# Batch 0's output product as seven half-size products, another order of its units, two later loads, and scores over 128 rows

## The chip, the cores and the metric

The kernel runs on one core of a Trainium2 chip. The metric is the device time of one execution in microseconds (us). TensorE (PE) multiplies matrices, VectorE (DVE), ScalarE (ACT) and GpSimd (POOL) work elementwise, and SyncE (SP) issues most of the DMAs. Each of them works through its own instructions in the order of the program.

## What is computed

```python
mask = q_bucket[:, :, :, None] == k_bucket[:, :, None, :]   # 6 sign bits of q @ proj, of k @ proj
scores = np.where(mask, scale * q @ k.T, -1e9)
attn = softmax(scores) @ v                  # 4 batches, 8 heads, 768 x 64
x = attn.transpose(0, 2, 1, 3).reshape(3072, 512)
h = x @ w_in                                # 512 x 2048
out = (h * sigmoid(h)) @ w_out              # 2048 x 512
```

Everything is float32 at the edges; the kernel multiplies in float16.

## The kernel before

**Attention in slots.** Two heads make a pair, two pairs a quad (`Q`), four pairs a batch. Each head is cut into `NU = 9` score blocks, so the main loop (line 735) has 288 slots `w`, 72 to a batch. A slot first issues what earlier units left over (`flush`), then what the table `at` holds for it (`plan(w, fn)`), then a number of units of the second stage, then `av(w)` (the attention product of block w, four matmuls of 65 columns) and at last `score(w + 3)`, which fills one PSUM bank and has ACT take the exponential. The program order of a slot is the order on every engine.

**Masks.** The even head of a pair has its scaled q and k in rows 0 to 63 of `QKA[pair % 4]`, and the sign bits with one more row behind them in rows 64 to 70, so that its score matmul reads 71 rows (line 375). The odd head uses `QKB`, 128 rows, with zeros in the unused ones. `proj_unit` (line 282) makes the bits; from pair 8 on `bits_unit` (line 334) moves them with two SP DMAs for each head, before that with DVE copies of 13 rows. q and k of pairs 8 and later come by `load_blocks` (line 86): eight SP DMAs of 96 KB for a pair. DVE turns them (`block_unit`, line 252), POOL casts them (`cast_unit`, line 260, one cast for each head).

**Second stage.** Each batch's 768 tokens are cut into a block of 512 (`ci = 0`) and one of 256 (`ci = 1`). `mm1` (line 461) makes h for one group of columns; ACT takes a tanh and DVE makes g. For `ci = 1`, and for `ci = 0` in batches 1 to 3, the product with `w_out` is a Strassen-Winograd scheme of seven half-size products: `product` (line 518) runs n = 1, 2, 6, 5, 3, 7, 4 with one unit for each 128 tokens (eight matmuls of 256 columns), and `comb` (line 500) makes the four sums of g blocks: n = 1 and 2 on DVE, n = 3 and 4 on POOL while the scores run. Products 5 and 3 add onto product 6 in its bank, product 4 onto product 7. Batch 0's 512 tokens use `whole` (line 554) instead: for each of four token tiles one bank, four units of four 512-column matmuls with the plain `w_out16`.

**Combinations of the weights.** `w_unit` (line 181) makes them on POOL, each in two halves (the first holds k = 0 to 3 of the eight row blocks): n = 1, 2, 4 into tiles of their own (`wt`), n = 3 in place into `B12`, a quarter of `w_out16`. Product 7 reads `B12`. `whole` needs `B12` as it was loaded, so the n = 3 halves are planned at slots 157 and 160, before batch 1's product 7.

**The order of units.** `moe_list(b)` (line 613) puts batch b's units in order; what does not fit into the batch's own 72 slots goes to `late`. At slot 145, 217 and so on `moe_head` takes the first six late units, and at slot 155, 227 and so on the next list is made and spreads the remaining late units among the new `mm1` units. A running credit decides in which slots a unit is issued, about two in three. When a unit has sums attached (`then`), they are issued by `flush` in the next slot.

**PSUM.** The tag "s" has three banks. Scores use them in turn, and each open product of the second stage keeps one.

Worked through the loop, the slots that matter are these in the kernel before: loads of pairs 10 and 11 at slots 116 and 117, projection and bits of pairs 8 and 9 at 128, pair 8's first score issued in slot 141, k of pair 10 turned by DVE and cast by POOL at slot 153 (`block_unit`, two `cast_unit`), pair 11's casts at 159, `w_unit(3)` at 157 and 160, the small block's products 1 and 2 at 166 and 168 with its sums 4 and 3 on POOL in slot 169. Units of `whole` stand in sixteen slots from 113 to 160.

The lines that a sentence can't say:

```python
            eng = nc.gpsimd if n > 2 and scoring else nc.vector          # comb
...
        small[1] = then(small[1], (1, 4, al), (1, 3, al))                # sums 4, 3 after small product 2
...
        units = spread(first[:-3], late) + [big[0]] + first[-3:] + [big[1]]   # batch 1's list
```

Of the kernel before, what the change touches and what calls it, by code (L numbers as in the profile page):

```python
# [9 lines left out]
F32 = mybir.dt.float32  # L10
# [3 lines left out]
ALU = mybir.AluOpType  # L14
# [3 lines left out]
def kernel(  # L18
# [139 lines left out]
    for i in range(NSL):  # L158
        (nc.vector if i < 2 else nc.gpsimd).memset(QKB[i][0:64, :], 0.0)
    ident16 = cst.tile([P, P], F16, name="ident16")  # L160

# [159 lines left out]
    def bits_halves(p, par):  # L321
        t, r0 = ((QKA[p % NSL], 64), (QKB[p % NSL], 0))[par]
        for c in range(4):
            half, n = divmod(c, 2)
            x0 = n * S + half * HS
            r = slice(32 * c, 32 * c + NR)
            dst = t[r0 : r0 + NR, x0 : x0 + HS].rearrange("d (x c) -> d x c", c=P)
            if n == 1 and par == 1:
                nc.vector.tensor_scalar(out=dst, in0=bits[p][r, :, 0:P],
                                        scalar1=sc[r, 2:3], scalar2=None, op0=ALU.mult)  # L330
            else:
                nc.vector.tensor_copy(out=dst, in_=bits[p][r, :, 0:P])

    def bits_unit(pairs, i, par):
# [12 lines left out]
        for n in range(2):  # L347
            c = 32 * (2 * i + n)
            r = slice(c, c + NR)
            dst = t[r0 : r0 + NR, n * S : (n + 1) * S].rearrange("d (x c) -> d x c", c=CB)  # L350
            if n == 1 and par == 1:
                nc.vector.tensor_scalar(out=dst, in0=bits[pairs][r, :, 0:CB],
                                        scalar1=sc[r, 2:3], scalar2=None, op0=ALU.mult)
            else:
                nc.vector.tensor_copy(out=dst, in_=bits[pairs][r, :, 0:CB])
# [15 lines left out]
    def score(w):  # L371
        h, pts = parts(w)
        p, par = divmod(h, 2)
        t = QKA[p % NSL] if par == 0 else QKB[p % NSL]
        rows = slice(0, 65 + NBIT) if par == 0 else slice(0, P)
        sp = ps.tile([P, 512], F32, tag="s", name="s_ps", bufs=LEAD)
        for jt, c0, n, o0 in pts:
            nc.tensor.matmul(sp[:, o0 : o0 + n], t[rows, S + jt * P : S + (jt + 1) * P],  # L378
                             t[rows, c0 : c0 + n], start=True, stop=True)
        u = upl.tile([P, 512], F16, tag="u", name="u")  # L380
# [75 lines left out]
    def moe_units(b):  # L456
# [43 lines left out]
        def comb(ci, n, f):  # L500
# [10 lines left out]
            if n == 3:  # L511
                dst = dst[:, f]
            eng = nc.gpsimd if n > 2 and scoring else nc.vector
            eng.tensor_tensor(out=dst, in0=x, in1=y, op=op)  # L514
# [38 lines left out]

        def whole(t, part):

            if part == 0:
                banks[t] = ps.tile([P, DMODEL], F32, tag="s", name="o2_ps", bufs=3)
            op = banks[t]
            for ft in range(4 * part, 4 * part + 4):
                x = blk[0, ft // NK][:, t // 2, ft % NK, t % 2 * P : (t % 2 + 1) * P]  # L560
                nc.tensor.matmul(op, x, w_out16[:, ft, :],  # L561
                                 start=(ft == 0), stop=(ft == NFT - 1))
            if part == 3:
                o = ops.tile([P, DMODEL], F32, tag="osb", name="osb", bufs=3)
                nc.vector.tensor_scalar(out=o, in0=op, scalar1=half_g, scalar2=None,
                                        op0=ALU.mult)
                dst = out[b * S : (b + 1) * S, :].rearrange("(p t) n -> p t n", p=P)
                nc.sync.dma_start(out=dst[:, t, :], in_=o)

        def then(fn, *combs):  # L570
# [9 lines left out]
        second = [lambda grp=grp: mm1(1, grp) for grp in range(NFT // 2)]  # L580
        second[7] = then(second[7], (1, 1, al))
        if b == 0:
            big = [lambda t=t, part=part: whole(t, part) for t in range(4) for part in range(4)]
        else:
            big = [lambda n=n, t=t: product(0, n, t)
                   for n in (1, 2, 6, 5, 3, 7, 4) for t in range(2)]
            first[13] = then(first[13], (0, 1, lo))
# [25 lines left out]
    def moe_list(b):  # L613


        first, second, big, small = moe_units(b) if b else first_units
        if b == 0:
            units = first + spread(second, big[:8])
            late[:] = big[8:] + small
            return units  # L620
        units = spread(first[:-3], late) + [big[0]] + first[-3:] + [big[1]]
        for i, c in enumerate("ababaababababa"):
            units.append((second, big)["ab".index(c)][("ababaababababa"[:i].count(c)) + 2 * (c == "b")])
        late[:] = big[8:] + small
        return units

# [71 lines left out]
    for Q in range(2, NQUAD):  # L698
# [13 lines left out]
        for i in range(2):  # L712
# [3 lines left out]
            if Q + 1 < NQUAD:  # L716
                plan(w0 + (28 if Q == 3 else 8) + i, lambda p=2 * Q + 2 + i: load_blocks(p))
    for i, n in enumerate((1, 2, 4, 3)):
        for half in range(2):
            plan((104, 107, 110, 112, 146, 149, 157, 160)[2 * i + half],  # L720
                 lambda n=n, half=half: w_unit(n, half))
# [82 lines left out]
```

## Time and profile before

| | us |
|---|---|
| median of 3 runs | 300.5 (299.92 to 302.83) |
| the profiled execution, its own time | 300.23 |
| its span | 298.5 |
| PE busy | 290.8 |
| ACT, DVE, POOL busy | 217.1, 187.1, 171.4 |
| projection of pairs 8, 9 on PE (slot 128) | at 93.2 |
| first `mm1` unit of batch 1 (slot 155) | at 118.1 |
| last attention product on PE (slot 287) | at 240.8 |

A row of the timeline gives start and duration in us, the engine, the line, what is written from what, and in brackets the idle time of the engine ahead of it with what ended that. A matmul's duration contains its way through the array, so a busy PE isn't a PE at its peak: the pace is read from one start to the next. A row of a group gives count, busy time, mean ns of one, and the idle time ahead of it.

### The profile page before, as it was taken

Reading aid. Unit: us, or ns where it says so; the run is one execution under the profiler, and the core shown is the slowest. Engines: PE = TensorE matmul, PEld = TensorE weight load, DVE = VectorE, ACT = ScalarE, POOL = GpSimd, SP = SyncE. Lnnn points to the kernel's source line nnn. Section 1 sums busy time; section 2 is a strip of 40 time slices with the busy share of each in tenths; the row PEclk is TensorE's granted clock in tenths of the full one; section 3 lists DMA queues with packets and bytes.
Section 4 is the critical chain, followed back from the end, with each engine's and each line's share of the span. In section 5 each row is a group of like instructions: output and inputs, shape, how many; then the busy total and the mean of one; then the engine's idle time right before and its main releaser. Section 6 shows DMA issues by size and latency. Waiting matters only on the chain.

```text
span 298.5 us, 7620 instructions
## 1 busy us (share of the span) xinstructions
PE 290.8 (97%) x2934; PEld 197.9 (66%) x2934; DVE 187.1 (63%) x362; ACT 217.1 (73%) x408; POOL 171.4 (57%) x223
## 2 busy tenths in 40 slices
PE   8999999999999989999999999999999999999995
PEld 3676855555666745567666888656668787667884
DVE  4797939899787464855798446954555453324262
ACT  5887999989987766877887786868888862446310
POOL 6588999388998644999357991599212730000000
PEclk9999999999999999999999999999999999999999
DMA  7999999999889919842199226203020313010113
GB/s 205 243 261 198 165 132 134 219 194 153 129 142 166 162 43 247 127 98 49 48 190 124 50 64 165 78 21 52 18 47 18 46 29 105 20 53 2 36 55 123
DMA packets 105716, 32.91 MB, mean 110 GB/s; under 512 B 90768, under 2 KB 105168, under 8 KB 105680
## 3 DMA queue, kind: packets, MB, share of 16 engines
q1 hardware_dynamic: 101296, 28.22, 47.0%
q0 software_dynamic: 4224, 4.19, 9.1%
q8 instruction: 23, 0.38, 0.5%
q14 instruction: 13, 0.11, 0.1%
q10 hardware_dynamic: 160, 0.00, 0.0%
HBM read 27.27 MB, written 6.29 MB: 112 GB/s over the span
## 4 chain that ended last, share of the span: by engine, by line
PE 94%; ACT 2%; DVE 2%; DMA 1%; issue 0%; POOL 0%; SPq 0%; ACTq 0%; POOLq 0%
PE h_ps L475 27%; PE o_ps L531 20%; PE s_ps L378 20%; PE o_ps L410 12%; PE o_ps L561 5%; PE bp_ps L293 3%; PE tp_ps L197 2%; ACT u L381 1%; PE warm_ps L125 1%; PE bp_ps L237 1%; DMA qka<-bits 1%; DVE osb L543 1%; PE tp_ps L210 1%; ACT th L489 0%; PE o_ps L401 0%
## 5 line engine op out<-in xcount | busy, mean ns | idle before, releaser
L381 ACT ACTIVATE u<-s_ps 128x512 f16<-128x512 f32 x288 | 156.8, 608 | 30.1 <-PE s_ps L378 29.6
L475 PE MATMUL h_ps<-xT,win 128*128 128x512 f16 (+1 forms) x512 | 98.4, 325 | 0.0
L410 PEld LDWEIGHTS <-u 128*128 128x128 f16 x1152 | 66.9, 98 | 38.1 <-ACT u L381 9.2
L410 PE MATMUL o_ps<-vv,u 128*128 128x65 f16 x1152 | 82.4, 194 | 0.6 <-ACT u L381 0.4
L492 DVE SCALAR_TENSOR_TENSOR g<-th,h_ps 128x512 f16<-128x512 f32 x72 | 48.5, 678 | 41.6 <-ACT th L489 41.3
L475 PEld LDWEIGHTS <-win 128*128 128x128 f16 x512 | 49.9, 98 | 24.9 <-issue 0.4
L378 PE MATMUL s_ps<-qka 71*128 71x512 f16 x192 | 52.9, 327 | 1.7 <-DMA qka<-bits 1.2
L531 PEld LDWEIGHTS <-g 128*128 128x128 f16 x480 | 46.8, 98 | 10.4 <-issue 1.2
L378 PE MATMUL s_ps<-qkb 128*128 128x512 f16 x192 | 52.9, 326 | 0.2 <-ACT u L381 0.2
L489 ACT ACTIVATE th<-h_ps 128x512 f32<-128x512 f32 x72 | 43.7, 607 | 11.3 <-PE h_ps L475 7.8
L430 POOL TENSOR_TENSOR x_pr<-osum,rec 128x384 f16<-128x384 f32 x23 | 19.7, 858 | 42.8 <-DVE rec L429 41.8
L543 DVE SCALAR_TENSOR_TENSOR osb<-o_ps,osb 128x256 f32<-128x256 f32 (+1 forms) x35 | 18.7, 535 | 22.8 <-PE o_ps L531 21.6
L263 POOL TENSOR_SCALAR qka<-qk 64x1536 f16<-64x1536 f32 x15 | 22.0, 1465 | 17.5 <-DVE qk L258 10.7
L531 PE MATMUL o_ps<-wt,g 128*128 128x256 f16 x240 | 30.7, 272 | 0.1
L531 PE MATMUL o_ps<-wout,g 128*128 128x256 f16 x240 | 30.4, 272 | 0.3 <-DVE osb L543 0.3
L485 ACT ACTIVATE g<-h_ps 128x512 f16<-128x512 f32 x24 | 14.3, 597 | 18.5 <-PE h_ps L475 18.5
L514 DVE TENSOR_TENSOR g<-g 128x1024 f16<-128x1024 f16 x24 | 18.2, 771 | 10.2 <-PE o_ps L531 5.3
L263 POOL TENSOR_SCALAR qkb<-qk 64x1536 f16<-64x1536 f32 x15 | 22.1, 1471 | 1.2
L274 POOL TENSOR_TENSOR vsa<-v_sb 128x192 f32<-128x192 f32 x32 | 18.9, 591 | 0.0
L272 POOL CAST vv<-v_sb 128x384 f16<-128x384 f32 x32 | 16.7, 522 | 1.4 <-DMA v_sb<-in_v_dram 1.0
L378 PEld LDWEIGHTS <-qka 71*128 71x128 f16 x192 | 15.5, 97 | 2.1 <-POOL vs L277 1.3
L561 PE MATMUL o_ps<-wout,g 128*128 128x512 f16 x64 | 16.4, 378 | 0.3 <-ACT u L381 0.2
(84 smaller groups left out, 296.5 us busy)
## 6 DMA issues: line engine op xcount, KB each, us to landing
v_sb<-in_v_dram SPq DMA_DIRECT2D x15, 384.0 KB
out_dram<-osb SPq DMA_DIRECT2D x16, 256.0 KB
q_blk<-in_q_dram SPq DMA_DIRECT2D x40, 96.0 KB
k_blk<-in_k_dram SPq DMA_DIRECT2D x40, 96.0 KB
win<-in_moe_w_in_dram POOLq DMA_DIRECT2D x4, 512.0 KB, 9.1
wout<-in_moe_w_out_dram POOLq DMA_DIRECT2D x4, 512.0 KB, 7.2
out_dram<-osb SPq DMA_DIRECT2D x16, 128.0 KB
q_sb<-in_q_dram SPq DMA_DIRECT2D x5, 384.0 KB
```

The costliest lines, as they stand in the source:

```text
L263: nc.gpsimd.tensor_scalar(out=dst[rows, :], in0=qk32[p][rows, :], scalar1=CS, scalar2=1.0, op0=ALU.mult, op1=ALU.mult)
L274: nc.gpsimd.tensor_tensor(out=sa, in0=src[:, 0:3], in1=src[:, 3:6], op=ALU.add)
L378: nc.tensor.matmul(sp[:, o0 : o0 + n], t[rows, S + jt * P : S + (jt + 1) * P], t[rows, c0 : c0 + n], start=True, stop=True)
L381: nc.scalar.activation(out=u, in_=sp, func=AF.Exp, scale=ESC)
L410: nc.tensor.matmul(o_ps[h][:, c0 // P + i, :], u[:, o0 + i * P : o0 + (i + 1) * P], vv[:, jt, :], start=(not direct(h) and w % NU == 0 and ...
L430: (nc.vector if direct(h) else nc.gpsimd).tensor_tensor(out=x_pr[p][:, :, par * D : (par + 1) * D], in0=o[:, 0:NJ, 0:D], in1=rec[:, :, Non ...
L475: nc.tensor.matmul(hp[:, :, j, :], w_in16[:, dt, ft * P : (ft + 1) * P], xT[4 * b + dt][:, c0 : c0 + n] .rearrange("d (r c) -> d r c", r=2 ...
L489: nc.scalar.activation(out=th, in_=hp, func=AF.Tanh, scale=0.5)
L492: nc.vector.scalar_tensor_tensor(out=g, in0=th.rearrange("p r f c -> p r (f c)"), scalar=1.0, in1=hp.rearrange("p r f c -> p r (f c)"), op ...
L531: nc.tensor.matmul(op[:, t, :], x[:, k, t * P : (t + 1) * P], y[:, k], start=(first and k == 0), stop=True, skip_group_check=True)
L543: nc.vector.scalar_tensor_tensor(out=o, in0=op, scalar=half_g, in1=kept[ci, add], op0=ALU.mult, op1=ALU.add)
L561: nc.tensor.matmul(op, x, w_out16[:, ft, :], start=(ft == 0), stop=(ft == NFT - 1))
```

## The change

Batch 0's block of 512 tokens uses the seven products as the other batches do, with its sums on DVE (all four of them for that block). `whole` goes. Batch 0's list interleaves six product units with the second `mm1` units, its sums 1 and 2 hang on `mm1` units 3 to 6 of `ci = 1`, and the last eight product units and the small products go to `late` in a new order. `w_unit(3)` is planned at slots 153 and 157. The loads of pairs 10 and 11 go to slots 121 and 131. The score matmuls of the even heads read all 128 rows of `QKA`; rows 64 to 127 are zeroed at the start (one memset on DVE, one on POOL, two SP DMAs that copy zeros), and the bit copies into `QKA` take 7 rows instead of 13.

Worked through the loop, the new order puts product 1 at slots 113 and 118, product 2 at 122 and 127, sums 1 and 2 (four halves) behind slots 130 to 136, product 6 at 140 and 142, product 5 at 145 and 147, small product 1 at 148, product 3 at 150 and 152, small product 2 at 153 (its sums 4 and 3 on POOL in slot 154), product 7 at 157 and 160, product 4 at 166 and 168. From slot 171 on the two kernels have the same units.

```diff
@@ -157,6 +157,10 @@
         nc.vector.memset(VS[i // 2][:, i % 2, D:E1], float(NJ))
     for i in range(NSL):
         (nc.vector if i < 2 else nc.gpsimd).memset(QKB[i][0:64, :], 0.0)
+    nc.vector.memset(QKA[0][64:128, :], 0.0)
+    nc.gpsimd.memset(QKA[1][64:128, :], 0.0)
+    for i in range(2, NSL):
+        nc.sync.dma_start(out=QKA[i][64:128, :], in_=QKB[i][0:64, :])
     ident16 = cst.tile([P, P], F16, name="ident16")
 
     w_in16 = cst.tile([P, NDT, DFF], F16, name="win")
@@ -323,8 +327,9 @@
         for c in range(4):
             half, n = divmod(c, 2)
             x0 = n * S + half * HS
-            r = slice(32 * c, 32 * c + NR)
-            dst = t[r0 : r0 + NR, x0 : x0 + HS].rearrange("d (x c) -> d x c", c=P)
+            nr = NR if par else NBIT + 1
+            r = slice(32 * c, 32 * c + nr)
+            dst = t[r0 : r0 + nr, x0 : x0 + HS].rearrange("d (x c) -> d x c", c=P)
             if n == 1 and par == 1:
                 nc.vector.tensor_scalar(out=dst, in0=bits[p][r, :, 0:P],
                                         scalar1=sc[r, 2:3], scalar2=None, op0=ALU.mult)
@@ -346,8 +351,9 @@
             return
         for n in range(2):
             c = 32 * (2 * i + n)
-            r = slice(c, c + NR)
-            dst = t[r0 : r0 + NR, n * S : (n + 1) * S].rearrange("d (x c) -> d x c", c=CB)
+            nr = NR if par else NBIT + 1
+            r = slice(c, c + nr)
+            dst = t[r0 : r0 + nr, n * S : (n + 1) * S].rearrange("d (x c) -> d x c", c=CB)
             if n == 1 and par == 1:
                 nc.vector.tensor_scalar(out=dst, in0=bits[pairs][r, :, 0:CB],
                                         scalar1=sc[r, 2:3], scalar2=None, op0=ALU.mult)
@@ -372,11 +378,10 @@
         h, pts = parts(w)
         p, par = divmod(h, 2)
         t = QKA[p % NSL] if par == 0 else QKB[p % NSL]
-        rows = slice(0, 65 + NBIT) if par == 0 else slice(0, P)
         sp = ps.tile([P, 512], F32, tag="s", name="s_ps", bufs=LEAD)
         for jt, c0, n, o0 in pts:
-            nc.tensor.matmul(sp[:, o0 : o0 + n], t[rows, S + jt * P : S + (jt + 1) * P],
-                             t[rows, c0 : c0 + n], start=True, stop=True)
+            nc.tensor.matmul(sp[:, o0 : o0 + n], t[:, S + jt * P : S + (jt + 1) * P],
+                             t[:, c0 : c0 + n], start=True, stop=True)
         u = upl.tile([P, 512], F16, tag="u", name="u")
         nc.scalar.activation(out=u, in_=sp, func=AF.Exp, scale=ESC)
         ut[w] = u
@@ -510,7 +515,7 @@
                              4: (a12, a12, a11, ALU.subtract)}[n]
             if n == 3:
                 dst = dst[:, f]
-            eng = nc.gpsimd if n > 2 and scoring else nc.vector
+            eng = nc.gpsimd if n > 2 and scoring and (b, ci) != (0, 0) else nc.vector
             eng.tensor_tensor(out=dst, in0=x, in1=y, op=op)
 
         banks, kept = {}, {}
@@ -551,22 +556,6 @@
                 "(p t) n -> p t n", p=P)
             nc.sync.dma_start(out=dst[:, t0 : t0 + nt, :], in_=o)
 
-        def whole(t, part):
-
-            if part == 0:
-                banks[t] = ps.tile([P, DMODEL], F32, tag="s", name="o2_ps", bufs=3)
-            op = banks[t]
-            for ft in range(4 * part, 4 * part + 4):
-                x = blk[0, ft // NK][:, t // 2, ft % NK, t % 2 * P : (t % 2 + 1) * P]
-                nc.tensor.matmul(op, x, w_out16[:, ft, :],
-                                 start=(ft == 0), stop=(ft == NFT - 1))
-            if part == 3:
-                o = ops.tile([P, DMODEL], F32, tag="osb", name="osb", bufs=3)
-                nc.vector.tensor_scalar(out=o, in0=op, scalar1=half_g, scalar2=None,
-                                        op0=ALU.mult)
-                dst = out[b * S : (b + 1) * S, :].rearrange("(p t) n -> p t n", p=P)
-                nc.sync.dma_start(out=dst[:, t, :], in_=o)
-
         def then(fn, *combs):
 
             def unit():
@@ -579,11 +568,14 @@
         first = [lambda grp=grp: mm1(0, grp) for grp in range(NFT)]
         second = [lambda grp=grp: mm1(1, grp) for grp in range(NFT // 2)]
         second[7] = then(second[7], (1, 1, al))
+        big = [lambda n=n, t=t: product(0, n, t)
+               for n in (1, 2, 6, 5, 3, 7, 4) for t in range(2)]
         if b == 0:
-            big = [lambda t=t, part=part: whole(t, part) for t in range(4) for part in range(4)]
+            for grp, c in ((3, (0, 1, lo)), (4, (0, 1, hi)), (5, (0, 2, lo)), (6, (0, 2, hi))):
+                second[grp] = then(second[grp], c)
+            for i, c in ((4, (0, 4, lo)), (5, (0, 4, hi)), (6, (0, 3, lo)), (7, (0, 3, hi))):
+                big[i] = then(big[i], c)
         else:
-            big = [lambda n=n, t=t: product(0, n, t)
-                   for n in (1, 2, 6, 5, 3, 7, 4) for t in range(2)]
             first[13] = then(first[13], (0, 1, lo))
             for grp, c in ((0, (0, 1, hi)), (1, (0, 2, hi)), (3, (0, 4, lo)), (4, (0, 3, lo))):
                 second[grp] = then(second[grp], c)
@@ -615,13 +607,16 @@
 
         first, second, big, small = moe_units(b) if b else first_units
         if b == 0:
-            units = first + spread(second, big[:8])
-            late[:] = big[8:] + small
-            return units
-        units = spread(first[:-3], late) + [big[0]] + first[-3:] + [big[1]]
-        for i, c in enumerate("ababaababababa"):
-            units.append((second, big)["ab".index(c)][("ababaababababa"[:i].count(c)) + 2 * (c == "b")])
+            units, order = first, "babababaaaaabb"
+        else:
+            units = spread(first[:-3], late) + [big[0]] + first[-3:] + [big[1]]
+            order = "ababaababababa"
+        n = order.count("b")
+        mixed = {"a": deque(second), "b": deque(big[:n] if b == 0 else big[8 - n : 8])}
+        units += [mixed[c].popleft() for c in order]
         late[:] = big[8:] + small
+        if b == 0:
+            late[:] = big[6:8] + small[:1] + big[8:10] + small[1:2] + big[10:] + small[2:]
         return units
 
 
@@ -714,10 +709,10 @@
             for j in range(2):
                 plan(w0 + 18 + 9 * i + 2 * j, lambda p=2 * Q + i, j=j: v_unit(p, (j,)))
             if Q + 1 < NQUAD:
-                plan(w0 + (28 if Q == 3 else 8) + i, lambda p=2 * Q + 2 + i: load_blocks(p))
+                plan(w0 + {3: 28, 4: 13 + 9 * i}.get(Q, 8) + i, lambda p=2 * Q + 2 + i: load_blocks(p))
     for i, n in enumerate((1, 2, 4, 3)):
         for half in range(2):
-            plan((104, 107, 110, 112, 146, 149, 157, 160)[2 * i + half],
+            plan((104, 107, 110, 112, 146, 149, 153, 157)[2 * i + half],
                  lambda n=n, half=half: w_unit(n, half))
     for p in range(NPAIR):
         plan((30, 42, 58, 75)[p] if p < 4 else 2 * NU * (p + 1) + (2 if p % 4 == 3 else 9),
```

## The prediction

> **What bounds the kernel now.** I read the page first, then the groups with their shapes kept apart, then the timeline of each engine around the batch seam (95 to 137 us), where the change puts its units.
>
> ```profile
> PE 290.8 (97%) x2934; PEld 197.9 (66%) x2934; DVE 187.1 (63%) x362; ACT 217.1 (73%) x408; POOL 171.4 (57%) x223
> ```
>
> PE is the bound, and the chain of waits says so too (94% PE). A microsecond of PE work removed is a microsecond won; a microsecond in which PE waits is lost, since nothing later has slack to give it back.
>
> PE around slots 141 to 157 (start, duration):
>
> ```profile
> 105.13 0.28 PE L410 MATMUL o_ps<-vv,u 128*128 128x65 f16 x4
> 106.65 0.38 PE L378 MATMUL s_ps<-qka 71*128 71x512 f16 x1 [1.24 <-DMA qka<-bits]
> ...
> 116.26 0.28 PE L410 MATMUL o_ps<-vv,u 128*128 128x65 f16 x4
> ...
> 119.68 1.03 PE L561 MATMUL o_ps<-wout,g 128*128 128x512 f16 x4
> ```
>
> The largest wait after the start is the second row: pair 8's first score (slot 141) waits for its bits. Four attention matmuls otherwise take 0.12 from start to start, here 1.52: 1.40 lost. The third row is the attention product of slot 152, ending at 116.54 (I call that T); the last is the unit of slot 157, at T + 3.14.
>
> Why the bits are late, in SP's queue:
>
> ```profile
> 96.06 2.66 SPq L92 DMA_DIRECT2D q_blk<-in_q_dram  x4
> 98.82 2.65 SPq L92 DMA_DIRECT2D k_blk<-in_k_dram  x4
> ...
> 103.60 1.73 SPq L343 DMA_DIRECT2D qka<-bits  x2
> ```
>
> SP is still issuing pair 11's loads, planned for slot 117, when DVE has made the bits (about 95.6).
>
> DVE and POOL after T:
>
> ```profile
> 116.58 0.23 DVE L423 COPY vsum<-o_ps 128x65 f32<-128x65 f32 x1 [1.24 <-PE o_ps L410]
> ...
> 117.69 1.58 DVE L258 STREAM_TRANSPOSE qk<-k_blk 128x768 f32<-128x768 f32 x1
> ```
>
> ```profile
> 117.78 0.83 POOL L430 TENSOR_TENSOR x_pr<-osum,rec 128x384 f16<-128x384 f32 x1 [3.07 <-DVE rec L429]
> 119.44 1.47 POOL L263 TENSOR_SCALAR qka<-qk 64x1536 f16<-64x1536 f32 x1 [0.83 <-PE o_ps L410]
> 120.98 1.47 POOL L263 TENSOR_SCALAR qkb<-qk 64x1536 f16<-64x1536 f32 x1
> 122.53 2.14 POOL L186 TENSOR_TENSOR wout<-wt,wout 128x1024 f16<-128x1024 f16 x1
> ...
> 134.87 2.13 POOL L514 TENSOR_TENSOR g<-g 128x1024 f16<-128x1024 f16 x1
> 136.95 2.13 POOL L514 TENSOR_TENSOR gd<-g 128x1024 f16<-128x1024 f16 x1
> ```
>
> Slot 152 ends a head. DVE starts on it at T, then turns k of pair 10 until T + 2.7; POOL casts pair 10 only then and reaches the first half of `w_unit(3)` at 122.53, though it is planned for slot 157 (119.7). The second half, planned for slot 160, runs at 127.97. POOL is 3 to 6 us behind PE here. Before, nobody waits for it: `B12` is needed only by batch 1's product 7, in slot 220.
>
> **What the Trainium skill says.** Page "TensorE: Matmul & The Clock Gate", section "Step-by-step: what each phase is for": matmuls stay in program order, only weight loads are pulled ahead. The trace agrees: at 105.1 to 106.65 the next unit, which needs no bits, stands behind the waiting score. Section "LDWEIGHTS (loading the stationary operand)": the time goes by columns, not by rows; here 97 ns for 71 rows and for 128. Section "What's actually happening": after an idle window of about 3.4 us PE falls to half its clock, and it takes as much busy time to come back. The trace shows only the start: 512-column warm-up matmuls start 426 ns apart early and 215 later. Page "GPSIMD Engine Reference", section "4.1 Engine selection": two-input elementwise work is about twice as slow there as on VectorE; here 2.13 to 2.20 us against DVE's 0.77 for 128x1024.
>
> **The change, part by part.**
>
> *Products.* Out: 16 units of four 512-column matmuls, 0.86 each (from starts 216 ns apart): 13.82. In: 14 units of eight of 256 columns, 109 ns apart: 12.21. Gain 1.6. Their weight loads (98 ns) stay under 109.
>
> *Rows.* In the starts of all records, an even head's 512-column score holds PE 219 to 220 ns, an odd head's 215; 256 columns 113 and 108. If that is the change of row count, 192 matmuls by about 4.5 ns give 0.85. Bounds 0 (it belongs to the tile) and 1.0. The zero fill: DVE's 0.70 (QKB's memset) fits its idle 0.9 us before 4.96; POOL's 1.37 pushes the first v work from 5.07 to 5.46, needed at 9.2; the two SP DMAs, 0.4 MB at the 0.2 MB/us moved there, delay pair 2's loads by 2 us, which land by 16 for a transpose at 16.8. Without that cover up to 1 us would show. Seven rows instead of 13 cost DVE the same (time goes by columns). I take 0.
>
> *Loads.* Bits of pairs 8 and 9 now stand behind pair 10's loads (slot 121) only, not pair 11's. Pair 11's eight DMAs took 5.5 us of SP, so the first bits go out near 98 and land near 102, ahead of 105. Gain 1.4 (range 0.7 to 1.6). Late next: pair 11's loads end near 110, still ahead of slot 156, but batch 1's last two transposed x tiles (slots 135, 146) come behind them, near 115, as slot 155 needs them. If they are late, slot 155 waits instead of slot 157, within the wait below.
>
> *Evictions and sums.* DVE loses four evictions (0.68), gets six (0.69) and eight sums (0.77): +7.6 us over slots 122 to 148. In slots 131 to 136 it has three g blocks (0.68), three sums and a head's end (1.0), 5.4 us against PE's 4.7. Product 6 in slot 140 needs sum 2, whose last half I find done 8.5 us after slot 130 starts; PE arrives at 7.75 and reaches that half at 8.2. Cost 0.4 (0 to 1).
>
> *Banks.* From slot 148 to 152 product 6/5/3's bank and the small product's are both open, so scores have one bank. In slots 149 and 151, which have no unit, the score must wait until ACT has emptied the bank: 0.2 until the matmul is through plus 0.6 for the exponential, less the 0.12 of attention between: 0.7 each, 1.4 (0 to 2). Before, one bank at most was open for long.
>
> *Product 7.* This decides. It is batch 0's second unit in batch 1's list, slot 157, and its right operand is `B12` after `w_unit(3)`: k = 0 to 3 need the first half, k = 4 to 7 the second. POOL's queue after T now holds, in order: the head's x (0.83), two casts, the first half (slot 153), small product 2's sums 4 and 3 (slot 154, 2.1 each from start to start), the second half (slot 157). The first half ended at T + 8.1 before. Product 3's eviction (0.69), issued just before the head's end, delays DVE by some 0.55: T + 8.7. Then 2.08 + 2.08 + 2.14: T + 15.0. PE wants product 7 at T + 3.14 and its fifth matmul at T + 3.57. It waits 15.0 - 3.6 = **11.4 us**, in two pieces (5.5 and about 5.9) around four matmuls. Everything on PE stands behind it, so ACT and DVE run dry too. Bounds: 10.8 without the DVE delay, 12.2 if POOL's steps lose 0.1 to 0.2 each. The 2.1 is not lengthened by DVE: two such steps took 4.21 at 110.51 with DVE mostly idle.
>
> *Clock.* Two idle stretches of over 3.4 us: PE probably restarts at half clock. About 4 us so, half lost: 2, by a chance of about three quarters: 1.5 (0 to 2.5).
>
> Sum: 300.23 - 1.6 - 0.85 - 1.4 + 0.4 + 1.4 + 11.4 + 1.5 = 311.1. The profiled execution is 0.3 below the median, within the spread of the runs. I say 311.
>
> **Rivals.**
> 1. *Likeliest, 0.72:* as above, 308.5 to 315.
> 2. *Shorter queue, 0.12:* the small sums don't stand ahead of the second half. Then it ends at T + 10.8, PE waits 7.2, the clock costs 0.8: 306. Against it: `flush` of slot 154 comes before the plan of slot 157, and `comb` takes POOL for the small block.
> 3. *Not slower, 0.09:* POOL is through with both halves by slot 157, so product 7 waits for nothing. Place: the same queue; it decides once the second half ends by T + 3.6 rather than T + 15. Then 300.23 - 3.85 + 1.8 = 298.2, or 296.4 if neither banks nor sums cost anything. For it: POOL is idle for 3.07 before T. Against: the queue is in order, and the first half stands behind casts whose k is turned only after slot 152.
> 4. *Worse, 0.07:* the half clock stays longer, or the x tiles are later than the wait covers: 316 to 320.
>
> **How the numbers follow.** A measurement here can tell about 1% from no change. Rivals 1, 2 and 4 are slower by over 1%: 0.91. Of rival 3, 0.05 goes to faster by over 1% (296.4), 0.04 to within. The range 305 to 315 holds rivals 1 and 2 and the bounds of the unknown terms, and leaves out 3 and 4.
>
> **What would show it.** Waits of PE at the L531 matmul that reads wout's changed quarter, released by POOL L186, some 11 us in two pieces near 114 to 126, with slices of low PE beside it; ACT and DVE dry; matmuls at 426 ns for 512 columns after it. No wait for qka<-bits near 104. Even and odd scores at one pace. Score waits for ACT near slots 149 and 151. I am wrong if the second half of `w_unit(3)` ends before product 7 comes up, or if PE finds other work while product 7 waits.

## The result, and the profile after

The changed kernel takes 315.53 us (median of 6 runs, 313.58 to 319.46), the kernel before beside it 300.08 (6 runs). The ratio is 1.050, interval 1.042 to 1.058: slower, as forecast, but half a microsecond above the range. Medians and ranges here and below hold every execution, while the ratios leave out those that stand over 1.5% above the fastest of their kernel; without the one such execution (319.46) the changed kernel's median is 314.18. The profiled execution took 313.65 (span 311.9), before 300.23 (298.5): 13.4 more.

The first part of the page of the changed kernel:

```profile
PE 292.2 (94%) x2982; PEld 204.2 (65%) x2982; DVE 196.4 (63%) x372; ACT 218.1 (70%) x410; POOL 175.8 (56%) x224
```

PE has 1.4 us more busy time in a span 13.4 longer: nearly all of it is waiting, not work. PE's waits, longest first (us in total, times, longest):

```profile
PE o_ps L536 <- POOL wout L190: 10.9, 2, 5.7
PE s_ps L383 <- ACT u L386: 2.8, 7, 0.6
```

The row at the top is new; in the kernel before nothing on PE waited for POOL after the warm-up. Its place on PE, around product 7 (slots 157 to 160):

```profile
123.97 1.01 PE L536 MATMUL o_ps<-wout,gd 128*128 128x256 f16 x4 [5.72 <-POOL wout L190]
130.19 1.01 PE L536 MATMUL o_ps<-wout,gd 128*128 128x256 f16 x4 [5.21 <-POOL wout L190]
...
131.70 1.91 PE L480 MATMUL h_ps<-xT,win 128*128 128x512 f16 x4
133.40 0.43 PE L415 MATMUL o_ps<-vv,u 128*128 128x65 f16 x4
```

Two waits around four matmuls. From start to start they cost 5.88 and 5.52 us more than the matmuls ahead of them need, 11.4 together. The last two rows are the clock: four 512-column matmuls take 1.70 to the next start, 426 ns each, where 0.86 was usual. The releaser, POOL:

```profile
117.05 0.83 POOL L435 TENSOR_TENSOR x_pr<-osum,rec 128x384 f16<-128x384 f32 x1 [3.65 <-DVE rec L434]
...
121.80 2.12 POOL L190 TENSOR_TENSOR wout<-wt,wout 128x1024 f16<-128x1024 f16 x1
123.88 2.12 POOL L519 TENSOR_TENSOR g<-g 128x1024 f16<-128x1024 f16 x1
125.95 2.12 POOL L519 TENSOR_TENSOR gd<-g 128x1024 f16<-128x1024 f16 x1
128.03 2.12 POOL L190 TENSOR_TENSOR wout<-wt,wout 128x1024 f16<-128x1024 f16 x1
```

The order is the one that the prediction wrote down: the head's x, two casts (1.47 each from 118.70, left out here), first half, two sums, second half, and POOL doesn't rest between the casts and the end. PE starts at 123.97, as the first half ends, and at 130.19, as the second does. The windows view shows the rest of the core in that wait and after it (columns: us, then busy time of PE, PEld, DVE, ACT, POOL, then clock, DMA share, GB/s):

```profile
118.00:131.00 13.00, 2.07 (x12) 1.12 (x9) 2.49 (x3) 1.19 (x3) 11.28 (x6) 0.64 0.80 138
131.00:136.00 5.00, 5.00 (x35) 3.00 (x34) 1.72 (x2) 2.39 (x4) 0.00 (x0) 0.57 0.00 0
```

In 13 us POOL works 11.3 and all others run dry; in the next 5, PE is busy throughout at 0.57 of its clock.

The wait for pair 8's bits is gone. SP's queue now:

```profile
98.17 1.73 SPq L348 DMA_DIRECT2D qka<-bits  x2
...
104.73 2.71 SPq L92 DMA_DIRECT2D q_blk<-in_q_dram  x4
```

The bits go out at 98.17 (103.60 before), ahead of pair 11's loads. In return scores wait for their bank in slots 149 (at 111.01) and 151 (first row), and in a place that was not foreseen, slot 175 (last row):

```profile
113.28 0.38 PE L383 MATMUL s_ps<-qkb 128*128 128x256 f16 x2 [0.56 <-ACT u L386]
...
149.28 0.38 PE L383 MATMUL s_ps<-qkb 128*128 128x256 f16 x2 [0.56 <-ACT u L386]
```

**Where the 13.4 us come from**, by the start of each slot's exponential against the kernel before: -0.5 from the start on, -1.3 at slot 99, -2.9 at slot 144 (bits -1.4, products), -1.6 at slot 158 (bank waits), +10.8 at slot 160, +12.5 at 163, +13.2 at 180, +13.4 at the end. Slots 158 to 163 hold it.

### The profile page after: what moved, and what is told of

It reads as the page before. It is cut to its first block, busy times and chain, and to the rows that moved or that the text cites. A ratio compares the mean times of both kernels' runs of the same rounds, so it can differ in the third digit from the quotient of the medians.

```text
span 311.9 us, 7739 instructions
## 1 busy us (share of the span) xinstructions
PE 292.2 (94%) x2982; PEld 204.2 (65%) x2982; DVE 196.4 (63%) x372; ACT 218.1 (70%) x410; POOL 175.8 (56%) x224
## 4 chain that ended last, share of the span: by engine, by line
PE 89%; POOL 4%; DVE 3%; ACT 2%; issue 1%; DVEq 0%; POOLq 0%; ACTq 0%
PE h_ps L480 26%; PE o_ps L536 23%; PE s_ps L383 19%; PE o_ps L415 12%; PE bp_ps L297 3%; PE tp_ps L201 2%; ACT u L386 2%; POOL wout L190 1%; PE warm_ps L125 1%; DVE qk L262 1%; DVE osb L548 1%; DVE g L519 1%; PE tp_ps L214 1%; POOL g L519 1%; POOL gd L519 1%
## 5 line engine op out<-in xcount | busy, mean ns | idle before, releaser
L536 PEld LDWEIGHTS <-g 128*128 128x128 f16 x576 | 56.1, 98 | 13.9 <-issue 2.7
L383 PE MATMUL s_ps<-qka 128*128 128x512 f16 x192 | 52.9, 327 | 1.3 <-ACT u L386 1.3
L494 ACT ACTIVATE th<-h_ps 128x512 f32<-128x512 f32 x72 | 44.1, 612 | 11.4 <-PE h_ps L480 8.2
L536 PE MATMUL o_ps<-wt,g 128*128 128x256 f16 x288 | 37.0, 272 | 0.1
L548 DVE SCALAR_TENSOR_TENSOR osb<-o_ps,osb 128x512 f32<-128x512 f32 (+1 forms) x40 | 22.1, 553 | 23.5 <-PE o_ps L536 22.2
L536 PE MATMUL o_ps<-wout,g 128*128 128x256 f16 x288 | 36.6, 273 | 0.3 <-DVE osb L548 0.3
L519 DVE TENSOR_TENSOR g<-g 128x1024 f16<-128x1024 f16 x30 | 24.9, 844 | 9.4 <-ACT g L490 4.7
L536 PE MATMUL o_ps<-wout,gd 128*128 128x256 f16 x96 | 13.4, 288 | 10.9 <-POOL wout L190 10.9
L536 PEld LDWEIGHTS <-gd 128*128 128x128 f16 x96 | 9.9, 103 | 13.6 <-issue 11.8
L276 POOL CAST vv<-v_sb 128x384 f16<-128x384 f32 x32 | 17.7, 553 | 0.6 <-DMA v_sb<-in_v_dram 0.2
```

Source lines behind the costliest of these rows:

```text
L383: nc.tensor.matmul(sp[:, o0 : o0 + n], t[:, S + jt * P : S + (jt + 1) * P], t[:, c0 : c0 + n], start=True, stop=True)
L494: nc.scalar.activation(out=th, in_=hp, func=AF.Tanh, scale=0.5)
L536: nc.tensor.matmul(op[:, t, :], x[:, k, t * P : (t + 1) * P], y[:, k], start=(first and k == 0), stop=True, skip_group_check=True)
L548: nc.vector.scalar_tensor_tensor(out=o, in0=op, scalar=half_g, in1=kept[ci, add], op0=ALU.mult, op1=ALU.add)
```

## The experiments

All runs of a section's kernels were made beside the kernel before on one chip. In some executions a load of q or k, or the bits that stand behind such loads in SP's queue, come late, and PE waits for them. I call an execution late if its mean clock is under 0.997: this counts the executions in which PE ran at half its clock for a while after such a wait. In the profiles of other kernels waits of 2.31 to 4.01 us brought that, and one of 2.38 didn't. 27 of 148 executions of the kernel before are late. In kernels that keep product 7's wait the count says nothing: the half clock behind it puts every execution under 0.99.

### What product 7's wait is worth, and what it is made of

Before: 299.63 (27 runs).

**Second product matrix early.** The changed kernel with

```diff
-            plan((104, 107, 110, 112, 146, 149, 153, 157)[2 * i + half],
+            plan((104, 107, 110, 112, 146, 149, 150, 151)[2 * i + half],
```

> The changed kernel, with the two halves of w_unit(3) planned at slots 150 and 151 instead of 153 and 157, so that POOL reaches them ahead of pair 10's casts. Theory (product 7 waits for the second half behind POOL's queue): both PE waits released by POOL go, 11.4 us, and with them the half clock, 2.7 us as read from the profile of the change; 313.65 - 14.1 = 299.5 us, within 1% of the kernel before. Rival (the seven products themselves crowd DVE, banks and POOL): the wait only moves to the next unit, and the time stays above 305 us.

Measured 301.5 (299.4 to 305.75, 22 runs), ratio 1.003 (1.000 to 1.006). PE, then POOL, in its trace:

```profile
123.17 1.04 PE L536 MATMUL o_ps<-wout,gd 128*128 128x256 f16 x8
```

```profile
118.42 4.66 POOL L190 TENSOR_TENSOR wout<-wt,wout 128x1024 f16<-128x1024 f16 x2
```

Both halves now run ahead of the head's x (123.04) and the casts, and product 7 goes through in one group of eight without a wait. Two slot numbers are worth 14 us. But the rest of the change, with a forecast gain, gains nothing, and 8 of 22 executions are late: the two questions of the next groups.

**The two sums on DVE.** The changed kernel with small product 2's sums away from POOL:

```diff
-            eng = nc.gpsimd if n > 2 and scoring and (b, ci) != (0, 0) else nc.vector
+            eng = nc.gpsimd if n > 2 and scoring and b > 0 else nc.vector
```

> The changed kernel, with the two sums of batch 0's small product 2 on DVE instead of POOL, so that only the casts and the first half stand ahead of the second half. Theory: the second piece of the wait shrinks from 5.5 to about 1.6 us (2 x 2.08 less, plus at most 0.3), the first piece of 5.9 stays; time 3.9 to 6 us below the changed kernel, 308 to 311 us. Rival (product 7 waits for something else that ends at the same time): no change, 313 to 316 us.

Measured 309.93 (309.53 to 310.92, 4 runs), ratio 1.034 (1.029 to 1.039).

```profile
125.19 1.01 PE L536 MATMUL o_ps<-wout,gd 128*128 128x256 f16 x4 [6.25 <-POOL wout L190]
127.27 1.01 PE L536 MATMUL o_ps<-wout,gd 128*128 128x256 f16 x4 [1.06 <-POOL wout L190]
```

The second piece falls from 5.52 to 1.37 (start to start), the first is 6.42 for 5.88. So the two sums (4.2 us) stood ahead of the second half. The first piece, which is left, went only in the experiment above, where the halves run ahead of the head's x and the casts. That also refutes rival 2.

**PE kept busy in the wait.** 100 matmuls on the warm-up tile ahead of product 7's first (work that no output uses):

```diff
+            if (b, ci, n, t) == (0, 0, 7, 0):
+                for _ in range(100):
+                    nc.tensor.matmul(op[:, t, :], warm, warm[:, None, :].to_broadcast([P, 2, P]),
+                                     start=True, stop=True)
```

> The changed kernel, with 100 matmuls of 256 columns on a constant tile issued ahead of product 7's first matmul, into the bank that it then clears; they fill about 10.9 of the 11.4 us that PE waits. They do no work for the output. Theory (idle PE comes back at half clock): the wait itself stays, but matmuls after it run at full pace, and the time falls by about 2.5 us, to 311 us, with a smaller spread between runs. Rival (the slow pace after the wait is not from idleness, or costs nothing): the time stays at that of the changed kernel or grows.

Measured 312.48 (311.04 to 316.19, 6 runs), ratio 1.042 (1.036 to 1.048).

```profile
134.25 1.03 PE L480 MATMUL h_ps<-xT,win 128*128 128x512 f16 x4
135.12 0.28 PE L415 MATMUL o_ps<-vv,u 128*128 128x65 f16 x4
```

The first matmuls behind product 7's two pieces: product 7 comes as late as before, with the added matmuls from 121.29 to 132.2 in the place of the idle time, and four 512-column matmuls take 0.87, not 1.70. From slot 135 to slot 189 this kernel gains 3.1 us on the changed one; 0.7 of it is slot 175's bank wait, which is absent here. The half clock costs 2.4 to 2.5. This profiled execution (313.72) isn't faster as a whole because it lost 3.2 us earlier to late loads of q and k; the three fastest, 311.04 to 311.23, stand about 2.5 below the lower group of the next paragraph.

**The changed kernel again**, unaltered.

> The changed kernel unaltered, on the same chip as the three above, to compare with. Theory: 313.5 to 317.5 us; its runs scatter by some 3 us if the clock's return falls differently from run to run. Rival: within 0.5 us of each other.

Measured 315.82 (312.95 to 324.15, 6 runs), ratio 1.048 (1.042 to 1.055). With the first six it makes twelve executions in two groups: six from 312.95 to 314.36, six from 316.89 to 324.15, with nothing between. Both profiled ones are of the first group; the median falls in the gap. Something adds about 5 us, from one group's median to the other's, to half of the executions.

### The parts by themselves

Before: 300.33 (11 runs).

**128 rows alone**: the kernel before with the zero fill, the 7-row bit copies and `rows = slice(0, P)`.

> The kernel before with the 128 score rows alone (the matmul slices, the zero fill at the start with its two SP DMAs, and the 7-row copies). Theory: the score matmuls of even heads go from 221 to 216 ns and from 112 to 109, 192 of them, which is 0.8 us of PE time; before slot 72 the exponentials set the pace and hide it, so that 0.3 to 0.6 us is won. Rival (the two added DMAs push pair 7's k loads back, and the projection at slot 93 waits for them more often): median 0.5 to 2 us above before, with a larger share of executions whose clock falls below 0.997.

Measured 302.24 (299.45 to 307.23, 6 runs), ratio 1.004 (0.999 to 1.009); 3 of 6 late. DVE in the profiled one, of 307.23:

```profile
64.74 1.53 DVE L262 STREAM_TRANSPOSE qk<-q_blk 128x768 f32<-128x768 f32 x1 [4.86 <-DMA q_blk<-in_q_dram]
```

DVE stands idle for 4.9 us until a load of q lands, long after the start; PE waits 4.01 us behind it. No gain of rows is visible.

**Later loads alone**: the kernel before with

```diff
-                plan(w0 + (28 if Q == 3 else 8) + i, lambda p=2 * Q + 2 + i: load_blocks(p))
+                plan(w0 + {3: 28, 4: 13 + 9 * i}.get(Q, 8) + i, lambda p=2 * Q + 2 + i: load_blocks(p))
```

> The kernel before with the later loads of pairs 10 and 11 alone. Theory: PE's wait for the bits of pair 8 (1.40 us from start to start) goes, nothing else changes: 1.2 to 1.6 us below before, 298.2 us. Rival (the transposed tiles behind pair 11's loads come late for batch 1's first unit): within 0.5 us of before, with a PE wait of about 1 us near 118 us.

Measured 299.05 (298.35 to 300.34, 6 runs), ratio 0.996 (0.993 to 0.999); none late. This is the best version found.

**Early matrix, 71 rows**: the first experiment without zero fill and without the rows, so products and loads alone.

> The changed kernel with both halves of w_unit(3) at slots 150 and 151, with 71 score rows and no zero fill. Theory: the zero fill is free and the rows give 0.3 to 0.6 us, so this is 0.3 to 0.6 us above the same kernel with 128 rows (301.5 us median, fast cluster at 299.4 to 300.6). Rival (the zero fill's DMAs bring the late loads of pair 7): the cluster at 303.5 to 305.8 us thins out, and the median falls to 299.5 to 300.5 us.

Measured 299.88 (299.43 to 300.2, 6 runs), ratio 0.999 (0.996 to 1.002); none late, as the rival of this expectation had it. Against the later loads alone it is 1.2 us ahead at slot 144, which is what the products win, and 1.3 behind from slot 180 on: the bank waits take it back.

**Early matrix, one bank at a time**: the first experiment with product 3 moved ahead of small product 1.

```diff
-            late[:] = big[6:8] + small[:1] + big[8:10] + small[1:2] + big[10:] + small[2:]
+            late[:] = big[6:10] + small[:2] + big[10:] + small[2:]
```

> The changed kernel with both halves of w_unit(3) at slots 150 and 151 and product 3's two units ahead of small products 1 and 2, so that bank 2 closes before the small products open theirs. Theory: the score waits of 0.7 us each in slots 149 and 151 go (1.5 us), and product 3 waits up to 0.7 us for product 5's eviction in slot 148; 0.8 to 1.5 us below the kernel with w_unit(3) early alone. Rival (scores wait there for ACT itself, not for a bank): no change.

Measured 299.94 (299.22 to 305.1, 6 runs), ratio 1.000 (0.995 to 1.004); 2 of 6 late. The waits of slots 149, 151 and 175 go, but:

```profile
114.24 1.03 PE L536 MATMUL o_ps<-wout,g 128*128 128x256 f16 x8 [0.72 <-DVE osb L548]
```

Product 3 now waits for evictions, in three places that cost 1.8 us from start to start: one wait in the place of another. The gain I expected isn't there.

### The zero fill

Before: 299.95 (67 runs).

**The two DMAs alone**: the kernel before with

```diff
+    for i in range(2, NSL):
+        nc.sync.dma_start(out=QKA[i][64:128, :], in_=QKB[i][0:64, :])
```

> The kernel before with nothing but the two SP DMAs of the zero fill added at the start (they write rows 64 to 127 of two QKA tiles; the scores still read 71 rows). Theory (the added 0.39 MB in the queue pushes pair 6's and 7's loads back): a third to a half of the executions stand 2.5 to 5 us above the rest with a clock below 0.997, and the median is 0.5 to 3 us above before. Rival (something else of the row change does it): one execution in seven at most, as in before, and the same median.

Measured 303.0 (299.26 to 309.24, 22 runs), ratio 1.003 (1.000 to 1.006); 12 of 22 late, before 10 of 67. They alone lift the median by 3 us. The profiled execution (303.64) is a late one. DVE waits for a load of k, which it doesn't in the kernel before, and later PE for the bits of pair 8:

```profile
92.19 1.60 DVE L260 STREAM_TRANSPOSE qk<-k_blk 128x768 f32<-128x768 f32 x1 [2.29 <-DMA k_blk<-in_k_dram]
```

```profile
108.58 0.38 PE L380 MATMUL s_ps<-qka 71*128 71x512 f16 x1 [2.46 <-DMA qka<-bits]
```

The first costs PE 0.7 us at the next projection. The second is 2.62 from start to start, 1.22 more than before: SP issues these bits at 105.54, for 103.60. Behind it PE runs at half clock until 112.3, which costs about 1.2. Together that is the 3.1 us by which this execution is behind.

**Rows by memset**: the zeros of slots 2 and 3 written by DVE, in slots 16 and 19, in place of the DMAs, on the kernel before; then the same with the later loads, and with the changed kernel and the early matrix.

```diff
+    for i in range(2, NSL):
+        plan(10 + 3 * i, lambda i=i: nc.vector.memset(QKA[i][64:128, :], 0.0))
```

> The kernel before with the 128 score rows, but the third and fourth QKA tiles zeroed by DVE in slots 16 and 19 (0.70 us each) instead of by DMAs. Theory: no more late executions than before, and the rows' gain alone shows: 0.3 us below before, 0 to 0.6. Rival (the rows or the start's memsets bring the late loads): a third of the executions late as with the DMAs.

> The kernel before with the later loads of pairs 10 and 11 and the 128 rows zeroed without DMAs; no products. Theory: the two gains add, 1.2 + 0.3: 298.5 to 298.9 us, below both kernels. Rival: the same as the loads alone, 299.05 us.

> The changed kernel with both halves of w_unit(3) at slots 150 and 151, and without the zero fill's two DMAs (DVE zeroes the tiles in slots 16 and 19). Theory: all the change's parts without its two faults; score waits for banks take back what the products win, so that it stands at 299.3 to 299.9 us, 0.2 to 0.6 below its 71-row form, without late executions. Rival (late loads come from the products' other work): a third of the executions late.

Measured 301.73 (299.26 to 303.92, 22 runs, 5 late), ratio 1.005 (1.002 to 1.007); 299.76 (299.25 to 301.23, 22 runs, none late), ratio 0.997 (0.995 to 0.999); 300.86 (300.36 to 301.62, 14 runs, none late), ratio 1.001 (0.998 to 1.003). All three medians miss their forecasts, by 0.9 to 2.1 us. The late executions go back to the level of the kernel before (5 of 22), and with the later loads to none, but my placement cost time of its own. DVE in the second kernel:

```profile
23.77 0.70 DVE L671 MEMSET qka<- 64x768 uint32 x1 [0.22 <-issue]
24.50 1.29 DVE L201 COPY qk<-tp_ps 128x512 f32<-128x512 f32 x2
```

The memset stands ahead of copies that PE's next projection waits for, and the kernel falls behind the later loads alone by 1.3 us from slot 27 to 36. After that it gains 0.3 by the end (1.64 to 1.33): in this pair of profiles, that is what the rows are worth.

With the loads of pairs 10 and 11 in their later places, 0 of 48 executions are late without the two DMAs (loads alone, early matrix with 71 rows, and the last two kernels here), and 10 of 28 with them (early matrix, one bank). So the later loads take away the late executions that the kernel before has of its own, and the two DMAs bring others. What the kernel before waits for in its late executions no profile shows; most likely it is pair 8's bits, for which the rows by memset, with the loads in their old places, wait 2.31 us in their late profiled execution, though no load is late there.

### What is it in the two DMAs?

Nearly half of the executions of kernels with them were late (25 of 56), but the fill had not been taken out of the changed kernel alone, and how it acts was open. Before: 300.07 (43 runs).

**The changed kernel with 71 rows**, without the fill.

> The changed kernel with the 71 rows of before and without the zero fill; everything else of the change stays (products, order, loads, place of w_unit(3)). Theory (the zero fill's two DMAs put the changed kernel's median above the forecast by making half of its executions late): hardly an execution is late, the median comes down from about 315.6 to 313.5 (313 to 314), inside the forecast's range, with product 7's wait of 11 us unchanged. Rival (the changed kernel's spread belongs to its long wait and the clock after it): the median stays at 315 to 316, with as many late executions as before.

Measured 313.7 (313.27 to 314.77, 6 runs), ratio 1.045 (1.041 to 1.049). Its waits:

```profile
PE o_ps L533 <- POOL wout L186: 10.9, 2, 5.7
```

Product 7's wait is untouched, the upper group of executions is gone, and the median lies in the forecast's range, as expected. If half of the executions still belonged to the upper group, six in a row outside it would be a chance of 1 in 64. The rows, which go with the fill here, aren't the reason: the early matrix with 128 rows by memset has no late execution among 14.

**Two tiny DMAs**: the kernel before with the two DMAs cut to `[64:128, 0:16]`, 2 KB each.

> The kernel before with the two SP DMAs at the same place in the queue, but of 64 rows by 16 elements (2 KB each) in place of 64 by 1536 (192 KB each). Theory (it is the traffic of 0.4 MB at the start): late executions as in the kernel before, about 1 in 7, the median 300. Rival (it is two more entries in the queue, or just another program): late executions in about half of the runs, the median 302 to 303, as with the two large DMAs.

Measured 301.28 (298.61 to 305.47, 22 runs), ratio 0.999 (0.996 to 1.002); 9 of 22 late, before 10 of 43. A hundredth of the bytes, and more late than before, though in 22 executions chance brings as large a difference from 10 of 43 about once in eight. The profile says more. DVE waits for the same load of k as with the large ones:

```profile
DVE qk L260 <- DMA k_blk<-in_k_dram: 2.4, 1, 2.4
```

PE then waits 2.38 us for pair 8's bits, without a half clock, so this execution (301.82) isn't counted late. My theory, traffic, falls.

**The two large DMAs on POOL's queue** (`nc.gpsimd` for `nc.sync`).

> The kernel before with the two large DMAs issued by POOL on its own queue, behind its memsets, so that the bytes are the same and SP's queue issues nothing more. Theory (SP's queue is what becomes late): late executions about 1 in 7, the median 300. Rival (any added traffic at the start does it): about half late, the median 302 to 303. POOL's own issuing may cost up to 0.5 us at the start.

Measured 301.1 (299.28 to 303.94, 22 runs), ratio 1.003 (1.000 to 1.005); 4 of 22 late, no more than before. All the bytes, and in the profile no wait of DVE for a load, and 1.27 us for the bits as in the kernel before (1.24). This points to the two entries in SP's queue. The other profiles agree that these bring late loads. In nine kernels with the two entries (the changed kernel, the same again, the two sums on DVE, PE kept busy, early matrix, one bank, 128 rows alone, two DMAs, two tiny ones) DVE's longest wait for a load of q or k is 1.1 to 4.9 us in eight and nothing in one; in the eight without them it is 0.7 at most. That the bytes don't matter rests on two kernels, with one profile and 22 executions each. The median still stands 1.0 above; where that is lost I didn't find.

**Four DMAs**, each of the two twice.

> The kernel before with each of the two SP DMAs issued twice: the suspected cost is doubled. Theory (traffic on SP's queue at the start): at least as many late executions as with two (half or more), the median 303 or above, and the first blocks of q and k may now be late themselves, 1 to 2 us on every execution. Rival (the late executions are no matter of these DMAs): about 1 in 7 late, the median 300 to 301.

Measured 309.2 (307.35 to 311.93, 6 runs), ratio 1.030 (1.025 to 1.036). This is no clean doubling:

```profile
8.03 9.82 SPq L162 DMA_DIRECT2D qka<-qkb  x4
```

Two took 1.2 us of SP, four take 9.8: the second DMA writes what the first wrote, so SP very probably waits for the first to land. Pair 2's q is issued 10.0 us later than in the kernel before (17.89 for 7.91), and PE waits 5.4 for it. The difference, about 4.6 us, is cover, in which the 2 us that the prediction gave two DMAs would be hidden. But the cover isn't there in every execution. PE's waits in the profiles of PE kept busy and of the two sums on DVE, with the two DMAs of the change:

```profile
PE tp_ps L201 <- DMA q_sb<-in_q_dram: 0.8, 1, 0.8
```

```profile
PE tp_ps L201 <- DMA q_sb<-in_q_dram: 0.5, 1, 0.5
```

Both stand near 17 us, at the transposes of pair 2's q. Later on four entries do less than two here: with everything 6.8 us behind, DVE's longest wait for a load is 0.7 us.

How two entries at 8 us make loads late 50 to 85 us on is left open. SP isn't simply behind until then: it issues the same transposed tile of x at 34.38 in the kernel before and at 34.37 with the two DMAs. Its queue further on, before and with the two DMAs:

```profile
69.85 4.17 SPq L92 DMA_DIRECT2D q_blk<-in_q_dram  x4
```

```profile
70.44 7.72 SPq L92 DMA_DIRECT2D q_blk<-in_q_dram  x4
```

The same four loads of pair 8 take 7.7 us to issue in place of 4.2 (7.8 with the tiny ones, 4.1 with those on POOL); the four behind them are the shorter for it (2.8 for 6.1). Nor does it mark the late executions: the changed kernel's profiled one, of the lower group, has the same pattern (7.5 and 2.8), and the late one of the early matrix hasn't (4.8 and 5.4).

## Why the prediction was right and wrong

**Product 7: right**, 11.4 forecast and 11.4 in the trace, place, releaser and two pieces included (5.88 and 5.52 for 5.9 and 5.5, the other way round). It came out because POOL's queue was written down instruction by instruction. That it agrees to the tenth is luck: POOL ends the first half at T + 9.3 for T + 8.7, PE arrives at T + 3.4 for T + 3.1, and of the time between the two halves about 0.3 goes to the slow clock of the four matmuls. Rivals 2 and 3 fall with the same timeline.

**The zero fill: the step that failed.** "The two SP DMAs ... delay pair 2's loads by 2 us, which land by 16 for a transpose at 16.8 ... I take 0." In the profile of the change that holds for pair 2, though not in every execution (0.8 and 0.5 us in two other profiles). But the step asked only for the next load behind the DMAs, in one profiled execution. SP's queue further on has little slack: with the two entries DVE waits 1.1 to 4.9 us for a load of q or k in eight of nine profiles, and 25 of 56 executions are late (in four kernels with them: the early matrix, 128 rows alone, one bank, the two DMAs alone), for 27 of 148 before. In the changed kernel this lifts the median by 1.8 us (315.53 against 313.7 without the fill), and that is what lies beyond the range. PE's waits in the profiled execution don't show it, which was one of the good ones; DVE's do, by a wait for a load of k that the kernel before hasn't and that costs PE nothing there:

```profile
90.15 1.58 DVE L262 STREAM_TRANSPOSE qk<-k_blk 128x768 f32<-128x768 f32 x1 [1.54 <-DMA k_blk<-in_k_dram]
```

No execution of the upper group was profiled, so what these wait for is inferred from the other kernels. With half of the executions in that group it was also luck on which side of 315 a median of six fell. Rival 4's times, 316 to 320, came in five of the twelve executions, but it named another cause. The fill isn't the whole miss either: of the 4.5 us above 311 about 2.6 are in the profiled execution already, mostly sizes that follow.

**The clock: size off.** 1.5 forecast by a chance of three quarters, 2.4 to 2.5 measured. Each of the two waits brings it, and four matmuls between them run at half pace too. The Trainium skill, page "TensorE: Matmul & The Clock Gate", section "What's actually happening", gives about 3.4 us idle for the fall and as much busy time for the way back; here PE ran at half pace from 130.2 to about 134.7, and in two other kernels idle stretches of 2.46 and 2.31 us, shorter than the page's figure, brought the fall too. Full credit for the drop would have been the better value.

**Banks: size off.** 1.4 forecast; 0.79 and 0.72 in slots 149 and 151, as worked out (0.7 each). Beside them 0.45 and 0.30 in two slots nearby (105.88 and 116.00), and 0.72 in slot 175, where the units of both kernels are the same. Against 0.64 of such waits before, the net is 2.3. Why slot 175 meets an occupied bank is left open.

**Rows: size off.** The pace came out as worked out (221 to 216 ns for 512 columns, 112 to 109 for 256), but of 0.85 only 0.3 was won. The lag against the kernel before shrinks only once the MoE units fill PE; before slot 72, I argue, the exponentials set the pace and PE's gain is idle time.

**Products, bits, sums: right.** -1.2 to -1.3 for -1.6; -1.4 for -1.4 (later loads alone: 1.2); sum 2 held product 6 up by 0.1 for 0.4.

The profiled execution in terms of the sum: -1.3 products, -1.4 bits, -0.3 rows, -0.5 start (chance), +2.3 banks, +0.1 sum, +11.4 product 7, +2.5 clock, +0.6 left over: 13.4.

## What to carry to other kernels

Before a unit is moved to an earlier slot, write down the queue of the engine that makes its operand, instruction by instruction with measured steps: where that engine is behind already, a planned slot says nothing of when the operand is there, and two slot numbers were worth 14 us here. A DMA put ahead of a queue of loads with little slack is judged by how often executions are late, over twenty runs, or by the waits of the engine that reads these loads, however far behind, not by the next load in one profile. And work saved on PE is won only where PE sets the pace and the banks are free.

## What the runs showed of the hardware that was not expected

A single idle stretch of PE in the middle of the kernel is enough for the half clock, and it needn't be long. In the profiled execution of the early matrix (a late one, 304.62) PE waits for a projection behind a late load of k:

```profile
67.57 2.79 PE L297 MATMUL bp_ps<-qk,pw 128*32 128x512 f32 x16 [3.54 <-DVE g L497]
```

These sixteen take 2.72 to the next start (70.29), where the kernel before takes 1.43 (64.38 to 65.81), at a granted clock of 0.50 until 70.4: a wait of 3.5 costs 1.3 more than itself. With the two DMAs alone a stretch of 2.46 was enough (above): the four 512-column matmuls from 108.80 take 1.59 to the next start, where 0.86 is usual, at a granted clock of 0.50 from 110 to 112. With the rows by memset it was one of 2.31, while with the tiny DMAs one of 2.38 brought no slow matmul. So between 2.3 and 2.5 us it can fall either way here.

Two DMAs of 2 KB in SP's queue at 8 us were followed by a wait of DVE of 2.4 us for a load of k near 90 us, two of 192 KB there by one of 2.3, and two of 192 KB in POOL's queue by none (late executions: 9, 12 and 4 of 22). With one profile of each this points to the place in SP's queue and not to the bytes; by what path is open.
